# The first product of an MLP, in feature-block order for its first two token tiles

## The chip, the cores and the metric

The kernel runs on one core of a Trainium2 chip. The time is the device time of one execution in microseconds, and for comparisons the median of several. Of each kernel one execution was also recorded by the hardware profiler. All the durations below come from that execution. Its span is the time from its first to its last instruction.

## The reference

The input x has 2048 tokens of 640 features. A layer norm without weights gives xn, which feeds two branches whose results are added to x:

```
xn  = (x - mean) / sqrt(var + 1e-5)
A:   q, k, v = xn @ wqkv            32 heads of 20 features
     phi(t) = (t + 1 if t > 0 else exp(t)) + 1e-6
     o = phi(q) (sum over tokens of phi(k)^T v) / (phi(q) . sum over tokens of phi(k) + 1e-6)
     A = o @ wo
B:   gelu(xn @ w1 + b1) @ w2 + b2   1536 hidden features
out = x + A + B
```

Inputs, weights and output are bf16. The change touches only the layer norm of the first tokens and the first product of branch B, xn @ w1.

## The kernel before

**Tiles.** Tokens are cut into 16 tiles of 128, the 640 features into 5 blocks of 128 (DT, index k), the 1536 hidden features into 12 blocks of 128 (JT, index jb). `x_in` holds x with tokens on the partitions, `xn_tm` the normalized tokens in the same layout, and `xnT` the normalized tokens transposed, with features on the partitions, which is what the products read. `HG` holds gelu(xn @ w1 + b1), with hidden features on the partitions.

**One unit of the first product.** `h_unit(t0, n, jb)` (line 392) takes one PSUM bank from a ring of eight (`take`), multiplies the five feature blocks of W1's hidden block jb with n tiles of `xnT` (five matmuls of n × 128 columns, L396), and lets ScalarE write the gelu of the bank into `HG` (L400). It waits for the piece of W1 that holds block jb and for all n tiles. W1 is loaded in four pieces of 384 hidden columns (`dma_w1`, L272), so one piece makes three hidden blocks complete.

**The order by hand.** `plan` (L425 to L428) lists the units in the order in which TensorE runs them: tiles 0 and 1 alone for blocks 0 to 5, tiles 0 and 1 together, tile 2, then widths that grow as tiles come in: (3, 1) is tile 3 alone, (3, 2) tiles 3 and 4, (5, 3) tiles 5 to 7, (8, 4) tiles 8 to 11. At the marks "T1" and "T2" TensorE transposes tile 1 and tile 2. Tiles 0 and 1 are transposed in two parts in two PSUM banks (`transp2`), which ScalarE (three blocks, L342) and VectorE (two blocks, L343) copy to `xnT`. Tile 2 is transposed in one bank and copied by VectorE (L385). Tiles 3 to 15 are transposed by DMA (`xnT_dma`, L389, issued by SP).

**The layer norm.** For each tile VectorE takes statistics of each half of the 640 features (`ln_half`, L347), combines them (`ln_aggr`, L355), POOL raises the variance to the power −1/2 (L357), and VectorE normalizes (`ln_norm`, L369). Each engine runs its instructions in the order in which the program records them, and waits at an instruction for whatever it needs. So the order in which these calls are written is the order of VectorE's queue. `ln_rest` (L430) handles tiles 5 to 15: statistics of tile t + 1 ahead of the norm and the transpose of tile t. In it, after tile 7's transpose, SP also issues the loads of tiles 8 to 15.

**Start.** TensorE runs `filler` matmuls on constants until tile 0 is there: ten of 512 columns, six of 128, and after tile 0's transposes three more of 128. SP issues the early loads in the order x0, x1, W1 pieces 0 and 1, x2, x3, W1 piece 2, x4 and x5, W1 piece 3, x6 and x7. `b1_step` transposes the bias of the first product.

**After the first product** come the key and value statistics (L505 on), the query product (L591) and the output product (L715). TensorE runs these stages one after the other. The change doesn't touch them.

Of the kernel before, what the change touches and what calls it, by code (L numbers as in the profile page):

```python
# [6 lines left out]
ACT = mybir.ActivationFunctionType  # L7
P = 128
FP32 = mybir.dt.float32
BF16 = mybir.dt.bfloat16  # L10
# [102 lines left out]
def bass_parallel_sum__linear_attn_block__dense_activation_gelu__prompt_kernel(  # L113
    nc: bass.Bass, A_x, A_wqkv, A_wo, B_x, B_w1, B_b1, B_w2, B_b2, out):
    Batch, S, D = A_x.shape
# [25 lines left out]
    with contextlib.ExitStack() as es:  # L141
# [28 lines left out]
        b1c = sb("b1c", [P, JT], FP32)  # L170
        b2bc = sb("b2bc", [P, D], BF16)
        ident = sb("ident", [P, P], BF16)
        onesm = sb("onesm", [P, P], BF16)
        hmask = sb("hmask", [P, 3, H], BF16)
        maskKV = sb("maskKV", [P, 2, WD], BF16)
# [38 lines left out]
        def halves(ap):  # L214
            return ap.rearrange("p (a n) -> p a n", a=2)

        r_x = [[R_("x%d" % t)] for t in range(NT)]
# [4 lines left out]
        W1P = [(i * F // 4, (i + 1) * F // 4) for i in range(4)]  # L222
        r_W1 = [R_("W1_%d" % i) for i in range(len(W1P))]
# [3 lines left out]
        r_b1tmp, r_b1c, r_b2 = R_("b1tmp"), R_("b1c"), R_("b2")  # L227
        r_ident, r_small, r_ones, r_masks, r_hmask = (
            R_("ident"), R_("small"), R_("ones"), R_("masks"), R_("hmask"))
        r_stats = [[R_("stats%d_%d" % (i, h)) for h in range(2)] for i in range(4)]  # L230
# [24 lines left out]
        FW = [next(i for i, (lo, hi) in enumerate(W1P) if jb * P < hi) for jb in range(JT)]  # L255

        g = "gpsimd"
        v = "vector"
# [3 lines left out]
        def dma(eng, dst, src, writes, reads=()):  # L262
            Pl.ins(eng, lambda e: e.dma_start(dst, src), reads=reads, writes=writes, dma=True)
# [4 lines left out]
        def dma_x(t, n):  # L268
            dma("sync", x_in[:, t:t + n, :], xv[t * P:(t + n) * P, :].rearrange("(t p) d -> p t d", p=P),
                sum(r_x[t:t + n], []))  # L270

        def dma_w1(i):  # L272
            lo, hi = W1P[i]
            dma("sync", W1[:, :, lo:hi], w1v[:, :, lo:hi], [r_W1[i]])

        dma_x(0, 1)
        dma_x(1, 1)
        dma_w1(0)
        dma_w1(1)
        dma_x(2, 1)  # L280
        dma_x(3, 1)
        dma_w1(2)
        dma_x(4, 2)
        dma_w1(3)
        dma_x(6, 2)

        Pl.ins(g, lambda e: e.memset(onesm[:], 1.0), writes=[r_ones])
        Pl.ins(g, lambda e: e.memset(mhalf[:], -0.5), writes=[r_small])
        Pl.ins(g, lambda e: e.memset(ident[:], 0.0), writes=[r_ident])
# [38 lines left out]

        XA = 3 * P

        def transp2(t, b0, b1):
            for lo, hi, b in ((0, 3, b0), (3, DT, b1)):
                pT = bank(b).bitcast(BF16)
                Pl.ins(pe, [(lambda e, k=k, pT=pT, lo=lo: e.transpose(  # L334
                    pT[:, (k - lo) * P:(k - lo + 1) * P], xn_tm[:, t, k * P:(k + 1) * P], ident[:]))
                    for k in range(lo, hi)], reads=[r_xn[t][0 if lo == 0 else -1], r_ident], writes=[B_[b]])

        def copy2(t, b0, b1):
            tok = slice(t * P, (t + 1) * P)
            pA = bank(b0).bitcast(BF16)[:, 0:XA].rearrange("p (k q) -> p k q", q=P)  # L340
            pB = bank(b1).bitcast(BF16)[:, 0:D - XA].rearrange("p (k q) -> p k q", q=P)
            Pl.ins(s_, lambda e: e.activation(xnT[:, 0:3, tok], pA, ACT.Copy), reads=[B_[b0]], writes=[r_xnT[t][0]])  # L342
            Pl.ins(v, lambda e: e.tensor_copy(xnT[:, 3:DT, tok], pB), reads=[B_[b1]], writes=[r_xnT[t][1]])  # L343

        def ln_half(t, h):
            s = t % 4
            Pl.ins(v, lambda e: e.bn_stats(stats[:, s, 6 * h:6 * h + 6], x_in[:, t, h * HW:(h + 1) * HW]),  # L347
                   reads=r_x[t], writes=[r_stats[s][h]])
            if h == 0:
                Pl.ins(g, lambda e: e.tensor_single_scalar(stats[:, s, 2:3], stats[:, s, 2:3], D * EPS, ALU.add),  # L350
                       reads=[r_stats[s][0]], writes=[r_stats[s][0]])

        def ln_aggr(t):
            s = t % 4
            Pl.ins(v, lambda e: e.bn_aggr(aggr[:, s, :], stats[:, s, :]),  # L355
                   reads=r_stats[s], writes=[r_aggr[s]])
            Pl.ins(g, lambda e: e.tensor_tensor(out=rstd[:, t:t + 1], in0=aggr[:, s, 1:2], in1=mhalf[:], op=ALU.pow),  # L357
                   reads=[r_aggr[s], r_small], writes=[r_rstd[t]])

        def ln_stats(t):  # L360
            ln_half(t, 0)
            ln_half(t, 1)
            ln_aggr(t)

        def ln_norm(t):
            s = t % 4
            for i, r in enumerate(r_xn[t]):
                lo, hi = (0, D) if len(r_xn[t]) == 1 else ((0, XA), (XA, D))[i]
                Pl.ins(v, lambda e, lo=lo, hi=hi: e.tensor_scalar(  # L369
                    xn_tm[:, t, lo:hi], x_in[:, t, lo:hi], aggr[:, s, 0:1], rstd[:, t:t + 1],  # L370
                    ALU.subtract, ALU.mult),
                    reads=r_x[t] + [r_aggr[s], r_rstd[t]], writes=[r])
# [19 lines left out]
        def h_unit(t0, n, jb):  # L392
            b = take(1)
            w = n * P
            tok = slice(t0 * P, t0 * P + w)
            Pl.ins(pe, [(lambda e, k=k: e.matmul(  # L396
                bank(b, 0, w), W1[:, k, jb * P:(jb + 1) * P], xnT[:, k, tok],
                start=(k == 0), stop=(k == DT - 1))) for k in range(DT)],
                reads=[r_W1[FW[jb]]] + sum(r_xnT[t0:t0 + n], []), writes=[B_[b]])
            Pl.ins(s_, lambda e: e.activation(  # L400
                HG[:, jb, tok], bank(b, 0, w), ACT.Gelu_apprx_tanh, bias=b1c[:, jb:jb + 1]),
                reads=[B_[b], r_b1c], writes=[r_HG[t][jb] for t in range(t0, t0 + n)])
# [2 lines left out]
               writes=[r_b1c])  # L405

        dma(s_, b1tmp[:], B_b1.rearrange("(a p) -> a p", p=P), [r_b1tmp])
        filler(10)
        filler(6, P)
        ln_half(0, 0)  # L410
        ln_half(0, 1)
        ln_aggr(0)
        ln_half(1, 0)
        ln_half(1, 1)
        ln_norm(0)
        b = take(2)
        transp2(0, b, b + 1)
        ln_aggr(1)
        copy2(0, b, b + 1)
        b1_step()  # L420
        filler(3, P)
        ln_norm(1)

        h_list = lambda t, n, lo, hi: [(t, n, jb) for jb in range(lo, hi)]
        plan = h_list(0, 1, 0, 3) + ["T1"] + h_list(0, 1, 3, 6) + h_list(1, 1, 0, 6)  # L425
        plan += h_list(0, 2, 6, 7) + ["T2"] + h_list(0, 2, 7, 9) + h_list(2, 1, 0, 9) + h_list(0, 3, 9, JT)
        plan += h_list(3, 1, 0, 3) + h_list(4, 1, 0, 3) + h_list(3, 2, 3, JT) + h_list(5, 3, 0, JT)
        plan += h_list(8, 2, 0, 3) + h_list(10, 2, 0, 3) + h_list(8, 4, 3, JT) + h_list(12, 4, 0, JT)  # L428

        def ln_rest():  # L430
            def out(t):
# [16 lines left out]
                out(t)  # L448

        for u in plan:  # L450
            if u == "T1":
                b = take(2)
                transp2(1, b, b + 1)
                copy2(1, b, b + 1)
                ln_stats(2)
                ln_half(3, 0)
                ln_half(3, 1)
                ln_norm(2)
                ln_aggr(3)
                ln_half(4, 0)  # L460
            elif u == "T2":
                b = transp(2)
                xnT_copy(2, b)
                ln_norm(3)
                xnT_dma(3)
                ln_half(4, 1)
                ln_aggr(4)
                ln_rest()
            else:
                h_unit(*u)  # L470
        run_masks(len(mask_jobs))
# [372 lines left out]
```

## Time and profile before

| | |
|---|---|
| median of 3 runs | 207.09 us (207.08 to 207.22) |
| profiled execution | 206.67 us |
| its span | 204.9 us |
| TensorE matmuls, busy | 200.1 us |
| VectorE, busy | 108.4 us |
| ScalarE, busy | 73.3 us |
| POOL, busy | 34.1 us |
| bytes moved by DMA | 21.14 MB |

In the profile PE is TensorE's matmul side and PEld its weight loads, DVE is VectorE, ACT ScalarE, SP the engine that issues most DMAs (SPq is its queue). L396 is line 396 of the kernel. A line of a timeline gives the start in us, the length in us, the engine, the line, the operation, output <- input and the number of instructions merged in it. A bracket at its end tells how long the engine stood idle before it, and what ended that wait. The row of 40 digits shows the busy share in tenths of 40 equal slices of the span, so one slice is 5.1 us. Matmuls overlap in the array: the duration of one is longer than the distance between two.

### The profile page before, as it was taken

What the parts mean: (1) busy time and instruction counts of PE and PEld (TensorE: products, weight loads), DVE (VectorE), ACT (ScalarE), POOL (GpSimd) and SP (SyncE); (2) the same over time, 40 slices, a digit from 0 to 9 for tenths busy, and PEclk for the clock granted to TensorE, in tenths of its full rate; (3) what the DMA queues carried; (4) which work ended last, traced back from release to release, by engine and by line L of the source; (5) the groups of instructions that cost most, each with busy time, mean ns of one, the idle gap of its engine ahead of it and who ended that gap; (6) DMA issues with size and microseconds to landing.
All of it is one profiled execution on the core that took longest, in us unless ns stands there. A gap on an engine that the chain in (4) does not pass through costs nothing.

```text
span 204.9 us, 3392 instructions
## 1 busy us (share of the span) xinstructions
PE 200.1 (98%) x1264; PEld 108.9 (53%) x1278; DVE 108.4 (53%) x236; ACT 73.3 (36%) x142; POOL 34.1 (17%) x85
## 2 busy tenths in 40 slices
PE   7899999999999999999999999999999999999995
PEld 3798767544444444444546444544444444447774
DVE  3784189100007898499758888534624824413322
ACT  2787877666676555121153554500000000000000
POOL 3342056810000000898000200000000000000000
PEclk9999999999999999999999999999999999999999
DMA  5956945897960111100010000228985422102111
GB/s 163 351 162 119 189 130 112 99 311 255 378 209 3 26 26 26 26 3 0 0 32 5 0 0 11 96 50 201 318 204 135 121 51 54 51 26 51 35 39 58
DMA packets 34233, 21.14 MB, mean 103 GB/s; under 512 B 19368, under 2 KB 34216, under 8 KB 34216
## 3 DMA queue, kind: packets, MB, share of 16 engines
q1 hardware_dynamic: 30736, 17.77, 32.6%
q10 hardware_dynamic: 3480, 3.15, 5.7%
q8 instruction: 10, 0.16, 0.4%
q14 instruction: 7, 0.06, 0.1%
HBM read 13.11 MB, written 2.62 MB: 77 GB/s over the span
## 4 chain that ended last, share of the span: by engine, by line
PE 95%; DVE 1%; DMA 1%; ACT 1%; issue 1%; DVEq 0%
PE ps L715 30%; PE ps L396 26%; PE ps L591 10%; PE ps L505 8%; PE ps L538 8%; PE ps L726 5%; PE ps L547 2%; PE ps L511 2%; DMA xPK<-in_A_x_dram 1%; DVE stats L347 1%; PE ps L601 1%; ACT Msb L627 1%; PE ps L655 1%; PE ps L334 0%; DVE xn_tm L369 0%
## 5 line engine op out<-in xcount | busy, mean ns | idle before, releaser
L396 PE MATMUL ps<-xnT,W 128*128 128x128 bf16 (+3 forms) x402 | 52.5, 292 | 0.2
L715 PE MATMUL ps<-W,HG 128*128 128x512 bf16 (+3 forms) x249 | 46.4, 338 | 0.3 <-ACT Msb L627 0.2
L400 ACT ACTIVATE HG<-ps,b1c 128x128 bf16<-128x128 f32 (+3 forms) x81 | 39.2, 517 | 14.3 <-PE ps L396 13.3
L396 PEld LDWEIGHTS ps<-xnT,W 128*128 128x128 bf16 x405 | 33.8, 98 | 18.4 <-DMA W<-in_B_w_dram 0.2
L715 PEld LDWEIGHTS ps<-W,HG 128*128 128x128 bf16 x252 | 24.0, 98 | 20.4 <-ACT Msb L627 0.2
L493 ACT ACTIVATE ek<-ps 128x512 bf16<-128x512 f32 x40 | 23.8, 598 | 19.3 <-PE ps L591 10.5
L494 DVE TENSOR_SCALAR ek<-ek 128x512 bf16<-128x512 bf16 x40 | 11.5, 288 | 28.3 <-ACT ek L493 28.3
L591 PE MATMUL ps<-xnT,Wqkv 128*128 128x512 bf16 x98 | 21.6, 379 | 0.1
L715 PE MATMUL ps<-Msb,PQ 128*128 128x512 bf16 (+3 forms) x104 | 20.8, 338 | 0.1
L347 DVE BATCH_NORM_STATS2 stats<-xPK 128x6 f32<-128x320 bf16 x32 | 14.0, 478 | 10.0 <-DMA xPK<-in_A_x_dram 9.9
L505 PE MATMUL ps<-Wqkv,xnT 128*128 128x512 bf16 x80 | 17.9, 379 | 0.0
L532 POOL COPY Wqkv<-Wqkv 128x128 bf16<-128x128 bf16 x25 | 14.0, 559 | 22.8 <-PE ps L511 21.3
L739 DVE TENSOR_TENSOR W<-ps,xnT 128x512 bf16<-128x512 f32 x12 | 8.3, 691 | 17.4 <-PE ps L715 11.5
L538 PE MATMUL ps<-xPK,xn_tm 128*128 128x512 bf16 x79 | 17.4, 379 | 0.1
L591 PEld LDWEIGHTS ps<-xnT,Wqkv 128*128 128x128 bf16 x100 | 9.7, 98 | 11.4
L496 DVE SCALAR_TENSOR_TENSOR PQ<-ps,ek 128x512 bf16<-128x512 f32 x20 | 13.8, 692 | 2.1
L715 PEld LDWEIGHTS ps<-Msb,PQ 128*128 128x128 bf16 x105 | 10.0, 98 | 8.4
L505 PEld LDWEIGHTS ps<-Wqkv,xnT 128*128 128x128 bf16 x80 | 7.8, 98 | 9.4
L538 PEld LDWEIGHTS ps<-xPK,xn_tm 128*128 128x128 bf16 x80 | 7.8, 98 | 9.4
L496 DVE SCALAR_TENSOR_TENSOR xPK<-ps,ek 128x512 bf16<-128x512 f32 x16 | 11.1, 692 | 1.7
L561 DVE TENSOR_TENSOR Msb<-Msb,xPK 128x640 f32<-128x640 f32 x14 | 11.6, 826 | 0.5
L357 POOL TENSOR_TENSOR rstd<-aggr,mhalf 128x1 f32<-128x1 f32 x16 | 9.9, 620 | 8.9 <-DVE aggr L355 8.9
(70 smaller groups left out, 113.6 us busy)
## 6 DMA issues: line engine op xcount, KB each, us to landing
Wqkv<-in_A_wqkv_dram SPq DMA_DIRECT2D x3, 800.0 KB, 6.8
W<-in_B_w_dram SPq DMA_DIRECT2D x4, 480.0 KB, 6.1
W<-in_B_w_dram SPq DMA_DIRECT2D x1, 1920.0 KB, 13.2
xnT<-in_A_x_dram SPq DMA_DIRECT2D x3, 512.0 KB, 5.5
xn_tm<-rden ACTq DMA_DIRECT2D x12, 128.0 KB, 4.5
out_dram<-W ACTq DMA_DIRECT2D x12, 128.0 KB, 1.7
xPK<-in_A_x_dram SPq DMA_DIRECT2D x4, 320.0 KB, 5.8
Wo<-in_A_wo_dram SPq DMA_DIRECT2D x8, 160.0 KB, 8.6
```

The source lines that it names most:

```text
L347: Pl.ins(v, lambda e: e.bn_stats(stats[:, s, 6 * h:6 * h + 6], x_in[:, t, h * HW:(h + 1) * HW]), reads=r_x[t], writes=[r_stats[s][h]])
L396: Pl.ins(pe, [(lambda e, k=k: e.matmul(bank(b, 0, w), W1[:, k, jb * P:(jb + 1) * P], xnT[:, k, tok], start=(k == 0), stop=(k == DT - 1))) ...
L400: Pl.ins(s_, lambda e: e.activation(HG[:, jb, tok], bank(b, 0, w), ACT.Gelu_apprx_tanh, bias=b1c[:, jb:jb + 1]), reads=[B_[b], r_b1c], wri ...
L493: Pl.ins(s_, lambda e: e.activation(e2, src, ACT.Exp), reads=br, writes=[r_ek[s]])
L494: Pl.ins(v, lambda e: e.tensor_scalar(et, et, 1.0, 1e-6, ALU.min, ALU.add), reads=[r_ek[s]], writes=[r_ek[s]])
L496: Pl.ins(v, lambda e: e.scalar_tensor_tensor(out=d2, in0=src, scalar=0.0, in1=e2, op0=ALU.max, op1=ALU.add), reads=br + [r_ek[s]], writes= ...
L505: Pl.ins(pe, [(lambda e, k=k, b=b, t=t: e.matmul(bank(b), xnT[:, k, t * P:(t + 1) * P], Wqkv[:, k, D:D + MW], start=(k == 0), stop=(k == D ...
L532: Pl.ins(g, lambda e, k=k, i=i: e.tensor_copy(plain(Wqkv[:, k, D:2 * D], i), parts(Wqkv[:, k, 0:D], i)), reads=[r_Wq], writes=[r_Wk, r_WqP])
L538: Pl.ins(pe, lambda e, t=t, b=b, f=f, i=i: e.matmul(bank(b), xn_tm[:, t, f * P:(f + 1) * P], PK[:, t, 0:MW], start=(i == 0), stop=(i == NT ...
L561: Pl.ins(v, lambda e, t=t: e.tensor_tensor(out=zsum, in0=zsum, in1=PK[:, t, :], op=ALU.add), reads=[r_PK[t], r_PKr[t // CH], r_zsum], writ ...
L591: Pl.ins(pe, [(lambda e, k=k, j=j, b=b: e.matmul(bank(b), Wqkv[:, k, D + j * P:D + (j + 1) * P], xnT[:, k, cc], start=(k == 0), stop=(k == ...
L715: Pl.ins(pe, [(lambda e, i=i, x=x, bk=bk: e.matmul(bank(bk, 0, x[1] - x[0]), seq[i][0], seq[i][1][:, x[0]:x[1]], start=(i == 0), stop=(i = ...
```

## The change

- **W1 is loaded by rows.** Five loads, each one feature block k with all 1536 hidden columns, take the place of four loads of 384 hidden columns. Every hidden block of a feature block is then there after one load, and a full unit needs all five.
- **Tiles 0 and 1 run in k order.** The new `hk(t, n, jb, ks)` runs only the feature blocks `ks` of hidden block jb. All 12 hidden blocks of tiles 0 and 1 are held at once in 6 PSUM banks, two hidden blocks of two tiles of 128 columns in each. `plan` runs tile 0 over k = 0, 1, 2, then tile 1 over k = 0, 1, 2, then both tiles together over k = 3 and 4, each over all 12 hidden blocks. The gelus of two hidden blocks follow when their bank is complete.
- **The banks are written once with zeros first.** Six matmuls of 512 columns on a zero tile `zt` write the six banks, and the matmuls after that all add. They stand in the place of six of the ten wide fillers. The three fillers after tile 0's transposes are gone. `at(b)` sets the ring to a bank.
- **x0 comes in two loads,** of 384 and 256 feature columns. Its statistics are taken in the same two parts. Its norm, and the transposes and copies of tiles 0 and 1, are cut at 256 columns (`KA = 2`) instead of 384.
- **Order.** The second statistics half of tile 1 moves behind the norm of tile 0. At T1 the norm of tile 2 stands ahead of the statistics of tile 3, and tile 4's statistics stay whole, after the norm of tile 3.
- **The rest of the plan.** Tile 2 alone for blocks 0 to 5, tiles 2 and 3 together for blocks 6 to 11, tile 3 alone for blocks 0 to 5, then tiles 4 to 7, 8 to 11 and 12 to 15 in groups of four for all 12 blocks.

The diff, cut to its core:

```diff
...
             dma("sync", x_in[:, t:t + n, :], xv[t * P:(t + n) * P, :].rearrange("(t p) d -> p t d", p=P),
                 sum(r_x[t:t + n], []))
 
-        def dma_w1(i):
-            lo, hi = W1P[i]
-            dma("sync", W1[:, :, lo:hi], w1v[:, :, lo:hi], [r_W1[i]])
-
-        dma_x(0, 1)
+        def dma_w1(k):
+            dma("sync", W1[:, k, :], w1v[:, k, :], [r_W1[k]])
+
+        XA = 3 * P
+        for i, (lo, hi) in enumerate(((0, XA), (XA, D))):
+            dma("sync", x_in[:, 0, lo:hi], xv[0:P, lo:hi], [r_x[0][i]])
         dma_x(1, 1)
         dma_w1(0)
         dma_w1(1)
+        dma_w1(2)
         dma_x(2, 1)
+        dma_w1(3)
         dma_x(3, 1)
-        dma_w1(2)
+        dma_w1(4)
         dma_x(4, 2)
-        dma_w1(3)
         dma_x(6, 2)
 
+        Pl.ins(g, lambda e: e.memset(zt[:], 0.0), writes=[r_zt])
         Pl.ins(g, lambda e: e.memset(onesm[:], 1.0), writes=[r_ones])
         Pl.ins(g, lambda e: e.memset(mhalf[:], -0.5), writes=[r_small])
         Pl.ins(g, lambda e: e.memset(ident[:], 0.0), writes=[r_ident])
...
             Pl.ins(s_, lambda e: e.activation(b1c[:], bank(b).bitcast(BF16)[:, 0:JT], ACT.Copy),
                    reads=[B_[b]], writes=[r_b1c])
 
-        XA = 3 * P
+        KA = 2
+        TC = KA * P
 
         def transp2(t, b0, b1):
-            for lo, hi, b in ((0, 3, b0), (3, DT, b1)):
+            for lo, hi, b in ((0, KA, b0), (KA, DT, b1)):
                 pT = bank(b).bitcast(BF16)
                 Pl.ins(pe, [(lambda e, k=k, pT=pT, lo=lo: e.transpose(
                     pT[:, (k - lo) * P:(k - lo + 1) * P], xn_tm[:, t, k * P:(k + 1) * P], ident[:]))
...
 
         def copy2(t, b0, b1):
             tok = slice(t * P, (t + 1) * P)
-            pA = bank(b0).bitcast(BF16)[:, 0:XA].rearrange("p (k q) -> p k q", q=P)
-            pB = bank(b1).bitcast(BF16)[:, 0:D - XA].rearrange("p (k q) -> p k q", q=P)
-            Pl.ins(s_, lambda e: e.activation(xnT[:, 0:3, tok], pA, ACT.Copy), reads=[B_[b0]], writes=[r_xnT[t][0]])
-            Pl.ins(v, lambda e: e.tensor_copy(xnT[:, 3:DT, tok], pB), reads=[B_[b1]], writes=[r_xnT[t][1]])
+            pA = bank(b0).bitcast(BF16)[:, 0:TC].rearrange("p (k q) -> p k q", q=P)
+            pB = bank(b1).bitcast(BF16)[:, 0:D - TC].rearrange("p (k q) -> p k q", q=P)
+            Pl.ins(s_, lambda e: e.activation(xnT[:, 0:KA, tok], pA, ACT.Copy), reads=[B_[b0]], writes=[r_xnT[t][0]])
+            Pl.ins(v, lambda e: e.tensor_copy(xnT[:, KA:DT, tok], pB), reads=[B_[b1]], writes=[r_xnT[t][1]])
 
         def ln_half(t, h):
             s = t % 4
-            Pl.ins(v, lambda e: e.bn_stats(stats[:, s, 6 * h:6 * h + 6], x_in[:, t, h * HW:(h + 1) * HW]),
-                   reads=r_x[t], writes=[r_stats[s][h]])
+            cut = XA if t == 0 else HW
+            lo, hi = ((0, cut), (cut, D))[h]
+            Pl.ins(v, lambda e: e.bn_stats(stats[:, s, 6 * h:6 * h + 6], x_in[:, t, lo:hi]),
+                   reads=[r_x[t][min(h, len(r_x[t]) - 1)]], writes=[r_stats[s][h]])
             if h == 0:
                 Pl.ins(g, lambda e: e.tensor_single_scalar(stats[:, s, 2:3], stats[:, s, 2:3], D * EPS, ALU.add),
                        reads=[r_stats[s][0]], writes=[r_stats[s][0]])
...
         def ln_norm(t):
             s = t % 4
             for i, r in enumerate(r_xn[t]):
-                lo, hi = (0, D) if len(r_xn[t]) == 1 else ((0, XA), (XA, D))[i]
+                lo, hi = (0, D) if len(r_xn[t]) == 1 else ((0, TC), (TC, D))[i]
                 Pl.ins(v, lambda e, lo=lo, hi=hi: e.tensor_scalar(
                     xn_tm[:, t, lo:hi], x_in[:, t, lo:hi], aggr[:, s, 0:1], rstd[:, t:t + 1],
                     ALU.subtract, ALU.mult),
...
             Pl.ins(pe, [(lambda e, k=k: e.matmul(
                 bank(b, 0, w), W1[:, k, jb * P:(jb + 1) * P], xnT[:, k, tok],
                 start=(k == 0), stop=(k == DT - 1))) for k in range(DT)],
-                reads=[r_W1[FW[jb]]] + sum(r_xnT[t0:t0 + n], []), writes=[B_[b]])
+                reads=r_W1 + sum(r_xnT[t0:t0 + n], []), writes=[B_[b]])
             Pl.ins(s_, lambda e: e.activation(
                 HG[:, jb, tok], bank(b, 0, w), ACT.Gelu_apprx_tanh, bias=b1c[:, jb:jb + 1]),
                 reads=[B_[b], r_b1c], writes=[r_HG[t][jb] for t in range(t0, t0 + n)])
...
                writes=[r_b1c])
 
         dma(s_, b1tmp[:], B_b1.rearrange("(a p) -> a p", p=P), [r_b1tmp])
-        filler(10)
+        def at(b):
+            ring[0] = b
+
+        def hk(t, n, jb, ks):
+            b = jb // 2
+            o = (jb % 2) * 2 * P + t * P
+            tok = slice(t * P, (t + n) * P)
+            Pl.ins(pe, [(lambda e, k=k: e.matmul(
+                bank(b, o, o + n * P), W1[:, k, jb * P:(jb + 1) * P], xnT[:, k, tok],
+                start=False, stop=(jb % 2 == 1 and k == DT - 1))) for k in ks],
+                reads=[r_W1[k] for k in ks] + [r_xnT[u][0 if max(ks) < KA else 1] for u in range(t, t + n)],
+                writes=[B_[b]])
+            if DT - 1 in ks and jb % 2:
+                for i in range(2):
+                    Pl.ins(s_, lambda e, i=i, jb=jb - 1 + i: e.activation(
+                        HG[:, jb, tok], bank(b, i * n * P, (i + 1) * n * P), ACT.Gelu_apprx_tanh, bias=b1c[:, jb:jb + 1]),
+                        reads=[B_[b], r_b1c], writes=[r_HG[u][jb - 1 + i] for u in range(t, t + n)])
+
+        at(6)
+        filler(4)
+        for b in range(6):
+            Pl.ins(pe, lambda e, b=b: e.matmul(
+                bank(b), nc.const_aps.tensor(1.0, [P, P], BF16), zt[:].broadcast_to((P, 512)), start=True, stop=False),
+                reads=[r_zt], writes=[B_[b]])
+        at(7)
         filler(6, P)
         ln_half(0, 0)
         ln_half(0, 1)
         ln_aggr(0)
         ln_half(1, 0)
+        ln_norm(0)
         ln_half(1, 1)
-        ln_norm(0)
-        b = take(2)
-        transp2(0, b, b + 1)
         ln_aggr(1)
-        copy2(0, b, b + 1)
-        b1_step()
-        filler(3, P)
+        transp2(0, 6, 7)
+        copy2(0, 6, 7)
         ln_norm(1)
 
         h_list = lambda t, n, lo, hi: [(t, n, jb) for jb in range(lo, hi)]
-        plan = h_list(0, 1, 0, 3) + ["T1"] + h_list(0, 1, 3, 6) + h_list(1, 1, 0, 6)
-        plan += h_list(0, 2, 6, 7) + ["T2"] + h_list(0, 2, 7, 9) + h_list(2, 1, 0, 9) + h_list(0, 3, 9, JT)
-        plan += h_list(3, 1, 0, 3) + h_list(4, 1, 0, 3) + h_list(3, 2, 3, JT) + h_list(5, 3, 0, JT)
-        plan += h_list(8, 2, 0, 3) + h_list(10, 2, 0, 3) + h_list(8, 4, 3, JT) + h_list(12, 4, 0, JT)
+        k_list = lambda t, n, ks: [(t, n, jb, ks) for jb in range(JT)]
+        plan = k_list(0, 1, [0]) + ["B1"] + k_list(0, 1, [1]) + ["T1"] + k_list(0, 1, [2])
+        plan += k_list(1, 1, [0]) + k_list(1, 1, [1]) + k_list(1, 1, [2]) + ["T2"] + k_list(0, 2, [3, 4])
+        plan += h_list(2, 1, 0, 6) + h_list(2, 2, 6, JT) + h_list(3, 1, 0, 6) + h_list(4, 4, 0, JT)
+        plan += h_list(8, 4, 0, JT) + h_list(12, 4, 0, JT)
 
         def ln_rest():
             def out(t):
...
                 out(t)
 
         for u in plan:
-            if u == "T1":
-                b = take(2)
-                transp2(1, b, b + 1)
-                copy2(1, b, b + 1)
+            if u == "B1":
+                at(6)
+                b1_step()
+            elif u == "T1":
+                transp2(1, 6, 7)
+                copy2(1, 6, 7)
                 ln_stats(2)
-                ln_half(3, 0)
-                ln_half(3, 1)
                 ln_norm(2)
-                ln_aggr(3)
-                ln_half(4, 0)
+                ln_stats(3)
             elif u == "T2":
+                at(6)
                 b = transp(2)
                 xnT_copy(2, b)
                 ln_norm(3)
                 xnT_dma(3)
-                ln_half(4, 1)
-                ln_aggr(4)
+                ln_stats(4)
                 ln_rest()
+            elif len(u) == 4:
+                hk(*u)
             else:
                 h_unit(*u)
         run_masks(len(mask_jobs))
...
```

More of the change, by code (lines that the diff above doesn't have):

```diff
@@ L172, in bass_parallel_sum__linear_attn_block__dense_activation_gelu__prompt_kernel @@
         ident = sb("ident", [P, P], BF16)
+        zt = sb("zt", [P, 1], BF16)
         onesm = sb("onesm", [P, P], BF16)
@@ L215, in halves @@
             return ap.rearrange("p (a n) -> p a n", a=2)
-        r_x = [[R_("x%d" % t)] for t in range(NT)]
+        r_x = [[R_("x%d_%d" % (t, i)) for i in range(2 if t == 0 else 1)] for t in range(NT)]
         r_xr = [R_("xr%d" % c) for c in range(NC)]
@@ L221, in bass_parallel_sum__linear_attn_block__dense_activation_gelu__prompt_kernel @@
         r_xnT = [[R_("xnT%d_%d" % (t, i)) for i in range(2 if t < 2 else 1)] for t in range(NT)]
-        W1P = [(i * F // 4, (i + 1) * F // 4) for i in range(4)]
-        r_W1 = [R_("W1_%d" % i) for i in range(len(W1P))]
+        r_W1 = [R_("W1_%d" % k) for k in range(DT)]
         r_Wk = R_("Wk")
@@ L227, in bass_parallel_sum__linear_attn_block__dense_activation_gelu__prompt_kernel @@
         r_b1tmp, r_b1c, r_b2 = R_("b1tmp"), R_("b1c"), R_("b2")
+        r_zt = R_("zt")
         r_ident, r_small, r_ones, r_masks, r_hmask = (
@@ L254, in bass_parallel_sum__linear_attn_block__dense_activation_gelu__prompt_kernel @@
         wqv = A_wqkv.rearrange("(k p) n -> p k n", p=P)
-        FW = [next(i for i, (lo, hi) in enumerate(W1P) if jb * P < hi) for jb in range(JT)]
         g = "gpsimd"
```

## The prediction

> **What bounds the kernel now.** I read the page first: the engine shares, the 40 slices, the chain that ended last. PE is TensorE's matmuls.
>
> ```profile
> PE 200.1 (98%) x1264; PEld 108.9 (53%) x1278; DVE 108.4 (53%) x236; ACT 73.3 (36%) x142; POOL 34.1 (17%) x85
> ...
> PE   7899999999999999999999999999999999999995
> ...
> DMA  5956945897960111100010000228985422102111
> ```
>
> TensorE is busy 98% of a 204.9 us span; only the first slice and the last show room. The chain in order of time (start, length, what) says when its real work begins:
>
> ```profile
> 6.62 1.00 PE ps L396 x15
> ...
> 7.90 3.20 PE ps L396 x50
> ...
> 11.38 25.65 PE ps L396 x235
> ```
>
> From 6.62 us TensorE runs the first product without a stall; the key product's first matmul (L505) starts at 59.53 in the timeline. So the change gains only what it starts before 6.62, and loses every stall that it makes between there and 59.53. What can be late is in VectorE's timeline (start, length), which normalizes the tiles:
>
> ```profile
> 8.33 0.89 DVE L347 BATCH_NORM_STATS2 stats<-xPK 128x6 f32<-128x320 bf16 x2
> 9.32 0.21 DVE L355 BATCH_NORM_AGGREGATE aggr<-stats 128x2 f32<-128x12 f32 x1
> 9.44 0.83 DVE L347 BATCH_NORM_STATS2 stats<-xPK 128x6 f32<-128x320 bf16 x2
> 10.29 0.45 DVE L369 TENSOR_SCALAR xn_tm<-xPK,aggr,rstd 128x640 bf16<-128x640 bf16 x1
> ...
> 13.12 0.83 DVE L347 BATCH_NORM_STATS2 stats<-xPK 128x6 f32<-128x320 bf16 x2
> ...
> 17.98 0.45 DVE L369 TENSOR_SCALAR xn_tm<-xPK,aggr,rstd 128x640 bf16<-128x640 bf16 x1 [0.53 <-POOL rstd L357]
> ```
>
> These are the statistics of tile 2, its aggregate, the statistics of tile 3, the normalization of tile 2, the statistics of tile 5 (13.12) and the normalization of tile 7 (17.98). SP then transposes tiles 3 to 7 by DMA and loads tiles 8 to 15 behind them in the same queue (SP's timeline; below it, tile 7's transpose alone, issued at 18.7, with its time to landing):
>
> ```profile
> 12.51 7.47 SPq L266 DMA_TRANSPOSE xnT<-xn_tm  x5
> 20.03 2.56 SPq L263 DMA_DIRECT2D xPK<-in_A_x_dram  x3
> ```
>
> ```profile
> L266 SPq DMA_TRANSPOSE xnT<-xn_tm x1: 1276/1276/1276, 18.7 to 18.7; - x1
> DMA to landing us min/median/max: 4.0/4.0/4.0
> ```
>
> Tile 7 is transposed at 22.70 (18.70 + 4.0). Its first reader, the group of tiles 5 to 7, begins at 23.83: 1.13 us of slack. The transposes of tiles 4 to 6 land 2.6 us after issue; tile 7's met a stretch (20.5 to 22.5) in which the DMA engines moved only 39 GB/s.
>
> **The Trainium skill.** "TensorE: Matmul & The Clock Gate", section "Wait — 56ns, not 53.3ns?": a warm matmul's pitch is its columns over 2.4 GHz plus about 2.5 ns. The trace agrees: 25 matmuls of 512 columns take 5.40 us in the chain (L591), 216 ns each; I use 56, 109, 163 and 216 ns. The same page, "Why this matters for your kernels", advises against TensorE idle gaps above about 3 us, after which the clock halves; the largest gap here is 0.76 us and the clock row stays at 9, so the trace doesn't test it. "ScalarE: Activation LUTs", section "What ACT_TABLE_LOAD costs": back-to-back activations overlap by about 93 ns. Eight 451 ns copies in 2.77 us (L627) are a pitch of 331, an overlap of 120. "PSUM — Partial Sum Buffer", section "The four PSUM rules": a matmul without the first-in-group flag adds where the bank was written before; the six zero matmuls are needed for that, and no run here shows it yet.
>
> **The change part by part.**
>
> *Matmul count.* The first product goes from 405 matmuls to 366 over the same columns (36+36+24 by feature block, then 54 units of 5). 39 fewer at 2.5 ns is 0.1 us. The zero matmuls take the place of six of ten 512-column fillers, at the same width: nothing, hidden in the wait for tile 0. Their extra memset on POOL (0.1 us) delays only masks that are ready at 1.7 us.
>
> *Start.* x0 lands at 3.18 now. In two loads (0.46 us more on SP) I take its 384 columns at 3.05 and the rest at 3.5; the statistics end at about 3.97 instead of 4.10. Aggregate, POOL's power (0.57) and the norm follow as now; the norm (5.17 now) is no longer behind tile 1's second half, so about 5.04. Its first piece is 256 columns (0.34 for 0.378), two transposes stand for three, and ScalarE copies 256 columns instead of 384 (0.40 for 0.49): copy done at about 6.14, first matmul at 6.25. W1's first row block must land by then: the now 0.49 MB first piece lands at 6.43; 0.10 MB less at 350 GB/s is 6.15. Gain 0.3 to 0.4 us, if nothing later waits.
>
> *W1 by rows.* Same bytes in all, rows of 3,072 B for 768 B, which no row of the trace has. Slow end: today's landing curve by bytes queued (1.475 MB at 8.3, 2.46 at 11.2, 2.95 at 12.65). Fast end: 399 GB/s, the best microsecond of the trace (43 to 44), for 350. Tile 2, now behind three row blocks (1.67 MB), lands at 8.2 to 8.8 instead of 8.3; W1's last block (2.62 MB) at 11.0 to 11.75. The k passes need one block each, the last pass all five. TensorE may wait some tenths for each.
>
> *ScalarE.* Twelve gelus of 256 columns now come within 24×109 ns = 2.6 us. At 476−93 = 383 ns each ScalarE needs 4.6 us; bank 5 is free about 5.3 us after the last pass begins, where TensorE would want it after 4.3 (2.6 plus six units of tile 2 at 0.28): a stall of 1.0 us (0.7 with an overlap of 120).
>
> *TensorE's arrival at the wide units.* Last pass from 11.7, so 17.0 at the group of tiles 2 and 3 (tile 3 transposed at 16.1, below), 6×0.547 + 6×0.28 = 5.0 more: 22.0. Without any of these waits 20.4. There stands (4,4), which reads tiles 4 to 7 at once; before, single units of tiles 3 and 4 and nine of tiles 3 and 4 together came first, and tile 7 was wanted at 23.83. This is the step that counts.
>
> *VectorE's chain to tile 7.* In its order, tile 2's statistics now stand behind tile 1's transposed copy, which waits for TensorE to finish two k passes: 6.25 + 0.67 + 0.07 + 0.67 = 7.66, 0.48 to the copy as now (7.46 to 7.94), 0.37 for its 384 columns: 8.5 at the earliest, 8.9 if the second row block or tile 2 is late. I take 8.65. Then the order changes: the norm of tile 2 comes before tile 3's statistics, so VectorE idles for POOL's power. From today's gaps: statistics to norm 1.96 (8.33 to 10.29), norm to the next 0.36, statistics to aggregate 0.99, aggregate to the copy of tile 2 about 0.12, norm of tile 3 at 4.28, tile 4's statistics at 4.63 (0.35 later), both halves and aggregate 1.10: tile 5's statistics begin 5.73 us after tile 2's. Now it is 13.12−8.33 = 4.79, since half of tile 4 and all of tile 3 filled those waits. So 8.65 + 5.73 = 14.38, 1.26 later than 13.12. From there nothing is changed: tile 7's transpose issues at 18.70 + 1.26 = 19.96 (behind tile 6's, 1.2 us of issue, as now), and lands at 23.96; tile 3's issues at about 13.4 and lands at 16.1.
>
> *Sum.* (4,4) starts at 24.0. Behind it are 36 units of 5×0.2158, 38.84 us: L505 at 62.85 instead of 59.53, so +3.3 us. All after that is TensorE-bound as before. TensorE's gains and waits ahead of 24.0 are hidden by this one wait of about 2 us; if that cover were gone they would set the arrival of 20.4 to 22.0. The profiled execution, 206.67 us (span 204.9 and 1.8 around it), becomes 210.0; on the median of 207.09 it is 210.4.
>
> **The rivals.**
>
> *The slow stretch doesn't hit tile 7.* Its 4.0 us isn't the rule: of the thirteen transposes ten took 2.5 to 2.7, and three 3.7 to 4.3. With 2.6 it lands at 22.6, and (4,4) starts at 22.6 to 22.9; the upper value is set by tile 11, transposed at 34.6 + 1.26 and wanted 60×0.2158 = 12.95 us after (4,4)'s start. +1.9 to +2.2 us: 209.0 to 209.3. For it: the stretch may be tied to a number of descriptors, which change. Against: the same issues follow each other, transpose 6, 7, loads of 8 to 15.
>
> *Clock.* If the rows land fast and TensorE comes at 21.0 or before, it idles 3 us there; the skill's rule would halve the clock for a window of some 3.4 us, 1.7 us more: about 212.1. Against it: some waits are spread, so I expect 2 us.
>
> *Not slower.* TensorE doesn't wait at (4,4): the earlier start then counts, with at best 0.4 + 0.1 us: 206.6. Place and price: tile 7 would have to be in by 20.7 (59.53 − 38.84), hence issued at 18.1 with 2.6 to landing, 0.6 us before today's issue, although VectorE comes to it later. It takes a load rate that today's trace doesn't show and a vector order without the 0.9 us of idling.
>
> **How the numbers follow.** Tile 7 late with the slow stretch: 0.52, 210.4, own range 209.8 to 211.2 (statistics of tile 2 between 8.5 and 8.9, with half a microsecond for unmeasured gaps). Without the stretch: 0.33. Clock: 0.08. Not slower: 0.05; other, small on both sides: 0.02. The range 208.7 to 211.4 holds the first two but for a small tail. A difference of 0.2% (0.4 us) is about what a measurement of this kernel tells from none. Slower 0.94, same 0.02, faster 0.04.
>
> **What would show it.** After: an idle stretch of TensorE of about 2 us ending near 24.0, at the first 512-column matmul of L396's line, released by a DMA into xnT; tile 7's normalization near 19.2; L505 first near 62.8; first product's matmul at about 6.25; VectorE waiting for POOL before tile 2's norm. I'm wrong if tile 7 is in by 21, or if TensorE comes to (4,4) later than 24, with ScalarE or a W1 block as the releaser.

## The result, and the profile after

The changed kernel takes 209.19 us (209.15 to 209.28), the kernel before 207.09: 1.0108 of it, with an interval of 1.0093 to 1.0123. It is 2.1 us slower. The profiled execution took 209.20 us, with a span of 207.5 us against 204.9.

The page of the changed kernel, the rows that were shown of before:

```profile
PE 202.3 (98%) x1236; PEld 105.7 (51%) x1236; DVE 108.6 (52%) x236; ACT 68.8 (33%) x127; POOL 34.0 (16%) x86
...
PE   8998799999999999999999999999999999999995
...
DMA  5934846697930111100010000318986411102012
```

TensorE's row has a 7 in its fifth slice (20.8 to 25.9 us), where before it had 9. TensorE's timeline of the changed kernel (start, length, line, what; the bracket is the idle time before it and what ended that):

```profile
6.69 0.83 PE L421 MATMUL ps<-xnT,W 128*128 128x128 bf16 x12 [0.24 <-ACT xnT L346]
...
8.24 0.44 PE L338 MATMUL ps<-ident,xn_tm 128*128 128x128 bf16 x5
8.52 2.84 PE L421 MATMUL ps<-xnT,W 128*128 128x128 bf16 x48
11.44 0.45 PE L383 MATMUL ps<-ident,xn_tm 128*128 128x128 bf16 x5
11.73 2.78 PE L421 MATMUL ps<-xnT,W 128*128 128x256 bf16 x24
14.35 1.63 PE L402 MATMUL ps<-xnT,W 128*128 128x128 bf16 x25
16.27 0.44 PE L402 MATMUL ps<-xnT,W 128*128 128x128 bf16 x5 [0.29 <-ACT HG L428]
17.00 5.11 PE L402 MATMUL ps<-xnT,W 128*128 128x256 bf16 x60 [0.29 <-ACT HG L428]
23.23 39.01 PE L402 MATMUL ps<-xnT,W 128*128 128x512 bf16 x180 [1.13 <-DMA xnT<-xn_tm]
62.08 4.48 PE L534 MATMUL ps<-Wqkv,xnT 128*128 128x512 bf16 x20
```

The groups of four (180 matmuls of 512 columns) start at 23.23 after 1.13 us of waiting for tile 7's transpose, and the key product starts at 62.08 instead of 59.53. In the kernel before, its line was:

```profile
59.53 4.48 PE L505 MATMUL ps<-Wqkv,xnT 128*128 128x512 bf16 x20
```

Those 2.55 us are the whole difference of the two profiled executions (2.53). A start of 59.53 would have needed the groups of four at 20.7 (their 180 matmuls take 38.84 us). TensorE came to them at 22.1, 1.4 later, and then waited 1.13. The 1.4 us are these differences between start times and work, read from the lines above: 0.2 in the first two k passes (1.55 us from 6.69 to 8.24 for 24×0.056 = 1.34, with the bias transposed between them), 0.2 ahead of tile 2's transpose (11.44 instead of 8.52 + 48×0.056 = 11.2), 1.0 behind the gelus (30 matmuls and their waits from 14.35 to 17.00 for 1.68), and 0.1 at the start, less 0.1 for fewer matmuls.

VectorE's timeline shows why tile 7 was late: the copy of tile 1, tile 2's statistics, aggregate and norm, tile 3's statistics, then the statistics of tile 5 and the norm of tile 7.

```profile
8.72 0.36 DVE L347 COPY xnT<-ps 128x384 bf16<-128x384 bf16 x1 [1.20 <-PE ps L338]
8.99 0.87 DVE L353 BATCH_NORM_STATS2 stats<-xPK 128x6 f32<-128x320 bf16 x2
9.97 0.21 DVE L361 BATCH_NORM_AGGREGATE aggr<-stats 128x2 f32<-128x12 f32 x1
10.94 0.45 DVE L375 TENSOR_SCALAR xn_tm<-xPK,aggr,rstd 128x640 bf16<-128x640 bf16 x1 [0.76 <-POOL rstd L363]
11.30 0.88 DVE L353 BATCH_NORM_STATS2 stats<-xPK 128x6 f32<-128x320 bf16 x2
...
14.72 0.83 DVE L353 BATCH_NORM_STATS2 stats<-xPK 128x6 f32<-128x320 bf16 x2
...
19.57 0.45 DVE L375 TENSOR_SCALAR xn_tm<-xPK,aggr,rstd 128x640 bf16<-128x640 bf16 x1 [0.53 <-POOL rstd L363]
```

VectorE waits 1.20 us for TensorE before tile 1's copy and 0.76 us for POOL before tile 2's norm. Tile 5's statistics begin at 14.72, 1.60 later than before (13.12), and so do all that follow. SP's queue, and tile 7's transpose alone with its time to landing:

```profile
13.73 7.86 SPq L266 DMA_TRANSPOSE xnT<-xn_tm  x5
21.64 0.58 SPq L263 DMA_DIRECT2D xPK<-in_A_x_dram  x1
```

```profile
L266 SPq DMA_TRANSPOSE xnT<-xn_tm x1: 1276/1276/1276, 20.3 to 20.3; - x1
...
DMA to landing us min/median/max: 2.7/2.7/2.7
```

It was issued at 20.31 and was in at 23.0: 2.7 us, not the 4.0 of the trace before.

### The profile page after: what moved, and what is told of

It reads as the page before. It is cut to its first block, busy times and chain, and to the rows that moved or that the text cites. A ratio compares the mean times of both kernels' runs of the same rounds, so it can differ in the third digit from the quotient of the medians.

```text
span 207.5 us, 3337 instructions
## 1 busy us (share of the span) xinstructions
PE 202.3 (98%) x1236; PEld 105.7 (51%) x1236; DVE 108.6 (52%) x236; ACT 68.8 (33%) x127; POOL 34.0 (16%) x86
## 4 chain that ended last, share of the span: by engine, by line
PE 91%; DVE 4%; DMA 1%; POOL 1%; issue 1%; ACT 0%; SPq 0%; DVEq 0%
PE ps L744 30%; PE ps L402 19%; PE ps L620 10%; PE ps L534 8%; PE ps L567 8%; PE ps L755 5%; PE ps L576 2%; PE ps L540 2%; DVE stats L353 2%; DMA xnT<-xn_tm 1%; PE ps L435 1%; PE ps L321 1%; POOL rstd L363 1%; DVE xn_tm L375 1%; PE ps L674 1%; PE ps L421 1%
## 5 line engine op out<-in xcount | busy, mean ns | idle before, releaser
L402 PE MATMUL ps<-xnT,W 128*128 128x512 bf16 (+2 forms) x270 | 46.2, 332 | 1.7 <-DMA xnT<-xn_tm 1.1
L402 PEld LDWEIGHTS ps<-xnT,W 128*128 128x128 bf16 x270 | 23.9, 98 | 23.6 <-issue 1.7
L406 ACT ACTIVATE HG<-ps,b1c 128x512 bf16<-128x512 f32 (+2 forms) x54 | 30.4, 612 | 15.9 <-PE ps L402 15.7
L744 PE MATMUL ps<-Msb,PQ 128*128 128x512 bf16 (+3 forms) x105 | 20.8, 338 | 0.0
L353 DVE BATCH_NORM_STATS2 stats<-xPK 128x6 f32<-128x320 bf16 (+2 forms) x32 | 14.0, 478 | 8.0 <-DMA xPK<-in_A_x_dram 8.0
L525 DVE SCALAR_TENSOR_TENSOR PQ<-ps,ek 128x512 bf16<-128x512 f32 x20 | 13.8, 692 | 2.1
L525 DVE SCALAR_TENSOR_TENSOR xPK<-ps,ek 128x512 bf16<-128x512 f32 x16 | 11.1, 692 | 1.7
```

The costliest lines, as they stand in the source:

```text
L402: Pl.ins(pe, [(lambda e, k=k: e.matmul(bank(b, 0, w), W1[:, k, jb * P:(jb + 1) * P], xnT[:, k, tok], start=(k == 0), stop=(k == DT - 1))) ...
L406: Pl.ins(s_, lambda e: e.activation(HG[:, jb, tok], bank(b, 0, w), ACT.Gelu_apprx_tanh, bias=b1c[:, jb:jb + 1]), reads=[B_[b], r_b1c], wri ...
L525: Pl.ins(v, lambda e: e.scalar_tensor_tensor(out=d2, in0=src, scalar=0.0, in1=e2, op0=ALU.max, op1=ALU.add), reads=br + [r_ek[s]], writes= ...
L744: Pl.ins(pe, [(lambda e, i=i, x=x, bk=bk: e.matmul(bank(bk, 0, x[1] - x[0]), seq[i][0], seq[i][1][:, x[0]:x[1]], start=(i == 0), stop=(i = ...
```

## The experiments

The theory after this result: two things, one behind the other, make the loss. TensorE loses 1.4 us ahead of the groups of four, and the groups of four ask for tile 7 while VectorE's changed queue has made that tile late. The rival: one of the two alone accounts for it. Each run was timed with the kernel before beside it; the ratios are to that.

**One part alone: the groups of four.**

```diff
 (in the plan of the kernel before)
-plan += h_list(3, 1, 0, 3) + h_list(4, 1, 0, 3) + h_list(3, 2, 3, JT) + h_list(5, 3, 0, JT)
-plan += h_list(8, 2, 0, 3) + h_list(10, 2, 0, 3) + h_list(8, 4, 3, JT) + h_list(12, 4, 0, JT)
+plan += h_list(3, 1, 0, JT) + h_list(4, 4, 0, JT)
+plan += h_list(8, 4, 0, JT) + h_list(12, 4, 0, JT)
```

> The kernel before with one part of the change alone: tile 3 alone for all 12 hidden blocks, then tiles 4 to 7 and 8 to 11 in groups of four. Theory (the groups of four ask for tile 7 before it is transposed): TensorE reaches them at 17.4 + 60 x 0.056 = 20.8 us and waits for tile 7, which came in at 22.7: about 1.9 us slower, 209.0 us; with a transpose of 2.6 instead of 4.0 us about 0.9 us slower, 208.0 us, bounded by tile 11. Rival (the loss comes from the front: zeroed banks, k order, gelus in a burst): 207.1 us.

Measured: 1.0138 (1.0102 to 1.0174). The interval is wide because three of six executions took 208.7 to 209.0 us and three 210.7 to 210.9. The first three are what the theory gave (209.0). The mean granted clock over the execution is 0.999 to 1.0 of full speed in these three and 0.992 in the other three, and the profiled execution is one of those. Its timeline and its stretches (columns: length, busy time of PE, PEld, DVE, ACT and POOL with their instructions, clock, DMA share, GB/s):

```profile
23.17 40.70 PE L396 MATMUL ps<-xnT,W 128*128 128x512 bf16 x180 [2.23 <-DMA xnT<-xn_tm]
```

```profile
23.40:23.70 0.30, 0.30 (x3) 0.18 (x2) 0.00 (x0) 0.00 (x0) 0.00 (x0) 0.93 1.09 358
23.70:24.00 0.30, 0.30 (x3) 0.04 (x2) 0.00 (x0) 0.00 (x0) 0.00 (x0) 0.50 1.05 371
24.00:26.50 2.50, 2.50 (x7) 0.87 (x6) 1.96 (x6) 0.69 (x1) 0.99 (x3) 0.50 0.91 290
...
27.00:27.30 0.30, 0.30 (x3) 0.17 (x2) 0.30 (x2) 0.10 (x1) 0.30 (x1) 0.88 0.31 115
```

After a wait of 2.2 us the clock fell to half, from 23.7 to 27.1, and the 180 matmuls took 40.70 us instead of 39.01. At half speed, 3.4 us of 209 are 0.8% less clock on average, which is the 0.992. This is the clock rival of the prediction, with a shorter wait than it supposed. Tile 7's transpose took 4.1 us here.

**The same with matmuls in the wait.** The edit adds `filler(18, 256)` ahead of `h_list(4, 4, 0, JT)`.

> The kernel before with tile 3 alone and groups of four, with 18 extra matmuls of 256 columns on constants (1.97 us) where TensorE waited for tile 7. Theory (the wait of over 2 us lets the clock fall to half for some 3 us in part of the executions, which costs the extra 2 us that three of six had): the clock stays full and all executions lie near 208.7 to 209.1 us. Rival (the slow executions come from something else, such as a later landing of tile 7): times from 208.7 to 210.9 us as without the matmuls.

Measured: 1.0124 (1.0110 to 1.0138), all four executions between 209.21 and 209.34 us, 0.1 above the theory's range (tile 7 was in at 23.1 in this profile, 22.9 in the one above), the clock at 9 in all slices. So in four executions the second group of times did not come when the wait was filled. The groups of four alone cost the kernel before about as much as the whole change does.

**The groups of four taken out of the change.**

```diff
-plan += ... + h_list(4, 4, 0, JT)
+plan += ... + h_list(4, 2, 0, JT) + h_list(6, 2, 0, JT)
```

> The changed kernel with tiles 4 to 7 in two groups of two instead of one of four. Theory: the wait of 1.1 us for tile 7 goes, 60 more matmuls cost 0.15 us: 208.1 to 208.2 us, still 1.0 us above the kernel before, for ScalarE's burst, the transpose of tile 2 and the start. Rival (the wait only moves on to tiles 8 to 11): 209.2 us.

Measured: 1.0085 (1.0072 to 1.0098), 208.50 us. The wait for tile 7 went, but the loads of tiles 8 to 15 stand behind its transpose, which took 4.3 us in this profile, and tiles 8 to 11 were late instead:

```profile
16.95 18.21 PE L402 MATMUL ps<-xnT,W 128*128 128x256 bf16 x180 [0.29 <-ACT HG L428]
35.49 26.06 PE L402 MATMUL ps<-xnT,W 128*128 128x512 bf16 x120 [0.34 <-DMA xnT<-xn_tm]
61.39 4.48 PE L534 MATMUL ps<-Wqkv,xnT 128*128 128x512 bf16 x20
```

So the theory held for the larger part (0.7 of the 1.0 us), and 0.34 us moved on, as the rival had it for all. In the kernel before the groups of four alone make 2 us of loss, with a transpose of tile 7 that took 4.1 us; in the change, without them, 1.8 us stay (208.50 beside 206.69). The two parts do not add up: either is enough for most of the loss.

**VectorE's order of before in the change.**

```diff
 copy2(1, 6, 7)
 ln_stats(2)
+ln_half(3, 0)
+ln_half(3, 1)
 ln_norm(2)
-ln_stats(3)
+ln_aggr(3)
+ln_half(4, 0)
 ...
 xnT_dma(3)
-ln_stats(4)
+ln_half(4, 1)
+ln_aggr(4)
```

> The changed kernel with VectorE's order of the kernel before at T1 and T2 (statistics of tile 3 ahead of the norm of tile 2, half of tile 4's statistics at T1). Theory (the new order idles VectorE for POOL and makes tile 7 late): tile 7 is transposed about 0.95 us earlier, near 22.0, TensorE's wait falls from 1.1 to 0.2 us: 208.2 to 208.3 us. Rival (TensorE's own late arrival at 22.1 sets the end, or the transpose of tile 7 takes 4.0 us at its new place): 209.1 to 209.3 us.

Measured: 1.0077 (1.0065 to 1.0089), 208.34 us. The changed kernel itself, run again, gives the comparison:

> The changed kernel unaltered, to have it on the same chip and beside the same runs of the kernel before as the three that follow: 1.0108 of the kernel before, 208.9 us where that takes 206.7. Its profile should show again a wait of about 1.1 us for tile 7's transpose; where the clock of TensorE comes up earlier than in the first profile, all up to tile 7 starts up to 0.4 us earlier.

Measured: 1.0122 (1.0109 to 1.0136), 209.22 us, 2.5 above the 206.73 of the kernel before beside it, with the same profile: the groups of four at 23.24 after 1.13 us. So the order brings 0.9 us, as expected. The groups of four in the kernel with the old order:

```profile
22.21 39.01 PE L402 MATMUL ps<-xnT,W 128*128 128x512 bf16 x180 [0.31 <-ACT HG L406]
```

No DMA releases them any more. But the path to it was half chance: in this profile the full clock came at about 4.4 us instead of after 6.1, so tile 2's statistics came at 8.48 instead of 8.99. From there to tile 5's statistics it took 5.22 us instead of 5.73. So of the 1.0 us by which tile 7's transpose was issued earlier (19.3 for 20.3) 0.5 are the order's, not 0.94, because VectorE now waits for the loads of tiles 3 and 4 (0.26 and 0.54 us).

**That order alone in the kernel before.**

> The kernel before with the change's order on VectorE alone (norm of tile 2 ahead of tile 3's statistics, tile 4's statistics whole). Theory: tile 7 comes in 0.9 us later, but the kernel before asks for it 1.1 us after it is in, so nothing is lost: 206.7 to 207.1 us, as the kernel before. Rival (the new order costs by itself): 207.6 us.

Measured: 1.0023 (1.0013 to 1.0032), 207.27 us. Both readings missed: it costs 0.5 us, where the theory had nothing and the rival 0.9. In its profile tile 7 is issued at 19.8 and takes 4.3 us. It is in at 24.1, when TensorE is ready for the groups of tiles 5 to 7, and they start at 24.36; the pair of tiles 10 and 11 (its last transpose issued at 33.4, 2.6 to landing) then waits until 36.09 too. The two places lose about 0.3 us each, so all of the 1.13 us of slack is used. That this profile's clock came up late (first matmul at 6.98) adds to the 207.53 us of that execution.

**TensorE's front and the fillers.** `filler(6, P)` becomes `filler(2, P)`.

> The changed kernel with two instead of six narrow fillers behind the zero matmuls. Theory A (TensorE's front feeds VectorE's queue through the transposed copy of tile 1, so it is on the way to tile 7): the transposes of tile 0 come 0.35 us earlier, and all up to tile 7 with them: 208.8 to 208.9 us. Theory B (as the prediction put it, TensorE's side ahead of tiles 4 to 7 is hidden by the wait for tile 7): 209.2 us.

Measured: 1.0106 (1.0093 to 1.0119), 208.91 us. In the profile the groups of four start at 22.86 instead of 23.23, after the same wait of 1.12. So theory A holds by the trace: TensorE's front moves VectorE's queue and tile 7 with it. The ratio by itself doesn't show it, since its interval meets those of the changed kernel.

**The burst.** VectorE's order of before, tile 2's transpose inside the last k pass, tile 3 transposed by TensorE, twelve units of tiles 2 and 3 instead of single tiles, and pairs ahead of the groups of four (the edits of VectorE's queue are left out here):

```diff
-plan += ... + ["T2"] + k_list(0, 2, [3, 4])
-plan += h_list(2, 1, 0, 6) + h_list(2, 2, 6, JT) + h_list(3, 1, 0, 6) + h_list(4, 4, 0, JT)
-plan += h_list(8, 4, 0, JT) + h_list(12, 4, 0, JT)
+last = k_list(0, 2, [3, 4])
+plan += last[0:4] + ["T2"] + last[4:8] + ["T3"] + last[8:JT]
+plan += h_list(2, 2, 0, JT) + h_list(4, 2, 0, 6) + h_list(6, 2, 0, 6) + h_list(4, 4, 6, JT)
+plan += h_list(8, 2, 0, 3) + h_list(10, 2, 0, 3) + h_list(8, 4, 3, JT) + h_list(12, 4, 0, JT)
```

> The changed kernel with VectorE's order of before, tile 2's transpose in the middle of the last k pass, tile 3 transposed by TensorE as well (0.28 us more there) and tiles 2 and 3 together in twelve units of two, then pairs ahead of groups of four. Theory (beside tile 7's wait, ScalarE's burst of twelve gelus costs 0.97 us and the wait for tile 2's norm 0.23): neither wait is left, 1.2 - 0.28 = 0.9 us less than with VectorE's order alone, about 1.003 to 1.004 of the kernel before. Rival (ScalarE's backlog only moves to later units): 1.007 to 1.008, as with VectorE's order alone.

Measured: 1.0030 (1.0018 to 1.0042), 207.26 us, as the theory had it.

```profile
6.68 0.83 PE L421 MATMUL ps<-xnT,W 128*128 128x128 bf16 x12 [0.34 <-ACT xnT L346]
...
14.67 45.67 PE L402 MATMUL ps<-xnT,W 128*128 128x256 bf16 x285
60.18 4.48 PE L542 MATMUL ps<-Wqkv,xnT 128*128 128x512 bf16 x20
```

From 14.67 on TensorE runs 285 matmuls without a wait. Neither ScalarE's backlog nor a late tile is left. The run changes several things at once, so what each of them brings is not shown. To the kernel before, 0.65 us remain (60.18 against 59.53). Tile 3's extra transpose (0.28) and the slow first passes (0.2) account for most of it.

**The start.** Next, the bias ahead of tile 0, and two narrow fillers:

> As after_burst, and with the bias transposed ahead of tile 0 and two narrow fillers instead of six. Theory (nothing waits any more, so the start counts in full): 0.1 us for the bias and 0.2 to 0.4 us for the fillers less than after_burst, 1.001 to 1.002 of the kernel before; 0.999 at best. Rival (the start is still hidden by a later wait): equal to after_burst.

Measured: 1.0027 (1.0014 to 1.0040), no gain. The rival holds, and the trace names the later wait, W1's rows:

```profile
6.17 1.50 PE L421 MATMUL ps<-xnT,W 128*128 128x128 bf16 x24 [0.22 <-ACT xnT L346]
...
8.28 2.85 PE L421 MATMUL ps<-xnT,W 128*128 128x128 bf16 x48 [0.30 <-DMA W<-in_B_w_dram]
11.53 1.03 PE L421 MATMUL ps<-xnT,W 128*128 128x256 bf16 x8 [0.40 <-DMA W<-in_B_w_dram]
```

TensorE starts half a microsecond earlier and gives it back at the third and the last row. How long it waits there is in part chance: the two rows landed at 8.24 and 11.40 here, and at 7.81 and 10.67 in the profile of the burst. Putting tile 2's transpose into the second of these waits:

> As after_burst2, with tile 2's transpose ahead of the last k pass, where TensorE waited 0.4 us for W1's last row, and tile 3's in its middle. Theory (the load of W1 now bounds the front, so that work put into its waits is free): 0.3 us less, 1.0012 to 1.0018 of the kernel before. Rival (tile 2's norm isn't there by then, or ScalarE's backlog comes back): 1.003 as after_burst2.

Measured: 1.0024 (1.0013 to 1.0034), short of the 1.0012 to 1.0018 of the theory. Tile 2's norm wasn't there at 11.1, so TensorE waited 0.21 us for that instead. None of these versions beats the kernel before.

**W1 by rows alone in the kernel before.**

> The kernel before with W1 loaded by rows, in the order of loads of the change, and nothing else: every unit of the first product needs all five rows. Theory: the last row lands at 10.9 us, so TensorE starts at 11.0 instead of 6.6: 4.3 us slower, and the idle stretch of over 4 us takes the clock to half for some 3 us, 1.5 to 2 us more: 212.7 to 213.5 us. Rival (the clock stays up): 211.0 to 211.3 us. Were rows no slower to use than pieces, 207.

Measured: 1.0304 (1.0287 to 1.0320), 213.27 us, as the theory said. The last row landed at 11.28, and TensorE's first product began at 11.64:

```profile
11.64 1.76 PE L396 MATMUL ps<-xnT,W 128*128 128x128 bf16 x15 [4.86 <-DMA W<-in_B_w_dram]
```

The clock was at half from 9.6 to 16.4. So rows without the k order would be worse than with it; the k order does hide most of the load.

**Tile 0's treatment alone in the kernel before.**

> The kernel before with the change's treatment of tile 0 alone: x0 in two loads, the cut at 256 columns, the norm of tile 0 ahead of tile 1's second statistics half. Theory (its start is bound by W1's first piece of 0.49 MB, which lands at 6.4 us or a little later now that a load stands before it, and by the clock's warm-up in the fillers): TensorE still starts at 6.6 to 6.9 us, 206.7 to 207.0 us, as before. Rival (tile 0 bounds the start): TensorE starts at 6.25, 0.4 us faster, 206.3 us. Tile 1's norm comes later behind the changed order, which may cost up to 0.2 us at T1.

Measured: 1.0000 (0.9991 to 1.0008). Tile 0's transposes came at 5.31 instead of 5.61, and the first product still began at 6.62. The time is what the theory said, but not for its reason. W1's first piece was in at 6.16, and the trace names VectorE's copy of tile 0 as the last wait:

```profile
6.62 1.00 PE L401 MATMUL ps<-xnT,W 128*128 128x128 bf16 x15 [0.29 <-DVE xnT L346]
```

That copy began at 6.17, behind the second half of tile 1's statistics and its aggregate.

## Why the prediction was right, and where it wasn't

The direction and the range (208.7 to 211.4) were right, and so was the place: the groups of four wait for tile 7's transpose. The likeliest time of 210.4 was 1.2 us too high, and the measured one lies in the range of the second case, to which I had given 0.33.

- **TensorE's arrival at the groups of four** was put at 22.0 and was 22.1, in part by luck. I had waits for W1's rows on the way; TensorE waited for none, and started 0.44 us later than put instead. ScalarE's burst was put at a stall of 1.0 us and cost 1.0. Twelve gelus took 4.48 us, a pitch of 361 ns, between the two that I had (383 and 356).
- **VectorE's chain.** From tile 2's statistics to tile 5's I had 5.73 us, and it took exactly that. Its start was 8.99 instead of 8.65, because tile 1's transposes came at 8.24 instead of 7.66: six wide zero matmuls and six narrow fillers ran to 5.7 on the half clock, which held longer in this execution than in the one before. The fillers stood in the way of tile 0's transposes, a step that I had costed at nothing.
- **The step that failed** is tile 7's time from issue to landing. I took the 4.0 us of the trace before, and it took 2.7. With 4.0 it would have been in at 24.3, and the kernel would have lost 1.3 us more. It is the rival "the slow stretch doesn't hit tile 7", with its 209.0 to 209.3. Smaller errors nearly cancel: tile 7 was issued 0.35 us later than put (20.31 for 19.96) and TensorE began 0.24 us after the landing, not 0.04; but I had added the loss to a median of 207.09, 0.4 above the profiled execution it was worked out from, while the changed kernel's two agree. Why the transpose took 2.7 us is taken up below.
- **"Hidden by this one wait"** was half right. TensorE's front is hidden where it only decides when TensorE arrives. But it also sets when VectorE gets on to tile 2, and so when tile 7 is in, as the run with fewer fillers shows.
- **The clock rival** did not come with the change, whose wait is 1.13 us. Its mechanism is real: it came in half the executions of the groups of four alone after a wait that was 2.2 us in the profiled one, where I had set the limit at 3.
- **The start** was put at 6.25 and was 6.69. An earlier start would probably not have brought the 0.4 us: in the bias and filler run, which started at 6.17, TensorE waited for W1's rows in the next passes.

**What goes with the 2.7 us.** Over all fourteen profiles, this transpose took 4.0 to 4.3 us in the six of the kernel before and its variants and in the pairs, and 2.7 in the other seven. The order of the loads doesn't account for it: W1 by rows alone in the kernel before had 4.0, x0 in two loads alone 4.1, and the pairs issue the same DMAs as the change. What goes with it stands in the DMA view (queue, kind: packets, MB, share of the 16 engines), taken from tile 7's issue to its landing, first before, then after:

```profile
q1 hardware_dynamic: 1338, 0.35, 91.9%
q8 instruction: 1, 0.02, 2.2%
```

```profile
q1 hardware_dynamic: 1335, 0.34, 67.8%
```

Beside tile 7's packets ran one transfer of 16 KB that the profile calls "instruction". In all seven profiles with 4.0 to 4.3 us such a transfer ran while the transpose was under way: it began at 19.8 to 20.0 us in the kernel before and four of its variants, at 26.9 with the rows (tile 7 issued at 25.6) and at 22.5 in the pairs (20.3). In six of the seven with 2.7 us none did (the changed kernel's next one began at 25.8), and in the burst one began 0.3 us before the landing. An early one seems to do little: in the run with x0 in two loads, tile 3's transpose (issued at 12.55) took 2.8 us with such a transfer from 12.7 to 13.8. Nothing in the prediction says where this load falls, so that it missed tile 7 in the change was luck. No run moves this load alone, so that it holds the transpose up is what the fourteen profiles agree on, not something tested.

## What to carry to other kernels

A saturated engine loses by any unit that asks for more tiles at once than have arrived. Before widening units, write down for each tile when it is in and when it is first asked for, and read how much slack the old order left (here 1.13 us). A queue on another engine that waits for the saturated one passes its delays on to tiles that come much later. And before you take the time of one slow transfer as its price, look in the DMA view for what else ran beside it.

## What the runs showed of the hardware

- **Half clock after a partial wait.** With the groups of four alone, three of six executions had a mean clock of 0.992; in the one of them that was profiled, TensorE had waited 2.2 us, and the clock stayed at half for 3.4 us (23.66 to 27.07). A wait of 4.9 us gave 6.8 us of it (9.63 to 16.45). A wait of 1.1 us gave none in the two profiles of the changed kernel, and its eight times lie within 0.3 us. "TensorE: Matmul & The Clock Gate" names about 3 us as the gap to avoid ("Why this matters for your kernels"); here less than that was too long. The half clock lasted 3.41 us and twice that, and the 2.2 us of waiting (20.94 to 23.17) lie in the 3.41 us just ahead of 23.66. That would fit a clock decided anew every 3.41 us, so that the same wait counts or doesn't by where it falls; two profiles suggest it, and no run tests it.
- **An instruction load beside a transpose.** Tile 7's transpose took 4.0 to 4.3 us from issue to landing in the seven profiles in which a 16 KB instruction load ran beside it and began 2 us or more before it landed, and 2.7 in the other seven.
- **Longer rows loaded faster.** From 6 to 11 us, W1 by rows of 3,072 B (with tiles of x between) moved at 355 to 409 GB/s in the changed kernel, and pieces with rows of 768 B at 336 to 362 in the kernel before. With the rows alone in the kernel before it was 390 from 8 to 10 us. The last of the tiles 0 to 7 landed at 12.7 instead of 13.4.
- **Warm-up.** At the start, matmuls of 512 columns follow each other every 427 ns, later every 216 to 220. With the same fillers up to there, the faster pace came between 3.4 and 3.7 us in the profile of the kernel before and after 6.1 in that of the groups of four alone. First products began at 6.62 and 6.92 there.
